# The order of the head in a fused state-space and SwiGLU kernel: when the first four row groups are normed, turned and sent through w1 and w3

## The chip, the cores and the metric

The kernel runs on one core of a Trainium2 chip. The metric is the device time of one execution in microseconds (us), as the median of three runs. A profile of one execution is read beside it.

The engines are named as in the profile: PE (TensorE, matmuls; PEld are its weight loads), DVE (VectorE), ACT (ScalarE), POOL (GpSimd), SP (SyncE, which here only issues DMAs). "L143" is line 143 of the kernel before.

## What is computed

```python
def _layernorm(x, axis=-1, eps=1e-5):
    m = jnp.mean(x, axis=axis, keepdims=True)
    v = jnp.var(x, axis=axis, keepdims=True)
    return (x - m) / jnp.sqrt(v + eps)

def reference(...):                      # x: 1 x 2048 x 512, bfloat16
    def _A_ref(x, ...):                  # diagonal complex state space, 512 states
        dt = jnp.exp(log_dt)
        Lam_bar = jnp.exp(dt * Lam)
        B_bar = ((Lam_bar - 1.0) / Lam)[:, None] * Bmat
        Bu = jnp.einsum("bld,pd->blp", x + 0j, B_bar)
        for t in range(L):
            h = Lam_bar[None, :] * h + Bu[:, t, :]
        ...
        return 2.0 * jnp.einsum("blp,dp->bld", hseq, Cmat).real + x * Dskip

    def _B_ref(x, w1, w3, w2):           # SwiGLU, 512 -> 1792 -> 512
        return (silu(x @ w1) * (x @ w3)) @ w2

    xn = _layernorm(x, axis=-1)
    return x + _A_ref(xn, ...) + _B_ref(xn, B_w1, B_w3, B_w2)
```

## The kernel before

The 2048 rows are cut into four blocks of 512 (`TBLK`), a block into four row groups of 128 (`CPB`; group c is "rows c" below). Every matmul needs the normed rows turned, with the 512 features on the partitions: `xnT` of a block is 128 x 4 x 512, where the 4 are the feature tiles (`NDT`).

The order of all engines' work is written out by hand (`manual_schedule`): each engine runs its instructions in the order of the text, and waits only for what they read or overwrite. From the second block on, VectorE's work stands in a queue of tasks with costs, and TensorE's loops call `drain(us)` to put as many of them between their own steps as fit. The norm of these blocks is such a task, and its turning is a transposing DMA.

Block 0 can't wait for that. Its head is the stretch that the change is about:

- SyncE's queue issues x of block 0 in three pieces (rows 0, rows 1, rows 2 and 3), then pieces of w1 and w3 (`load_w13`: f tiles 0 to 1, 2 to 3, 4 to 5, ...); the first w1 piece is on ScalarE's queue.
- `keep_warm` (L140) runs matmuls on a constant tile whose result nobody reads.
- For each row group: `stats` and `aggr` on VectorE (mean and variance), `rstd_act` on ScalarE (Ln, then Exp with -0.5: the reciprocal root), `normed` on VectorE (`xn`), `turn` on TensorE (four 128 x 128 transposes into PSUM), and `put`, which copies the turned rows out of PSUM into `xnT`, on ScalarE or VectorE.
- `ahead` (L491) runs the matmuls of the first three f tiles (`begun`: three gate and three up banks of PSUM) on those row groups that are there; a bank holds 512 rows of one f tile.
- `par_cols` (L256): TensorE turns the state-space parameters (`prm` into `pprm`), ScalarE copies them out and takes an Exp, GpSimd multiplies; then ScalarE takes `r_col` and loads the table that holds Silu (L527).

`glu_up(0)` (L361) then finishes the last 128 rows of the three begun f tiles, and goes on with f = 3 to 13 at the full width of 512 rows. For each f tile ScalarE takes Silu of the gate bank (`sl16`, L374) and copies the up bank (`up16`, L376), and VectorE multiplies them (L383). PSUM has eight banks, handed out in turn: the gate matmuls of f = 3 get the bank of the first begun tile and wait for its Silu. The first task that `glu_up(0)` drains is `par_turns` (L279), some 3 us of VectorE's work on the parameters.

The order of the head of before is L500 to L538, printed below.

Of the kernel before, what the change touches and what calls it, by code (L numbers as in the profile page):

```python
# [11 lines left out]
ALU = mybir.AluOpType  # L12
# [3 lines left out]
BF16 = DT.bfloat16  # L16
P = 128
# [3 lines left out]
def kernel(  # L21
# [24 lines left out]
    nc = tc.nc  # L46
    _, S, D = A_x.shape
# [5 lines left out]
    CPB = TBLK // P  # L53
    NSB = TBLK // SB
    NDT = D // P
    NPT = PS // P
# [7 lines left out]
    const = ctx.enter_context(tc.tile_pool(name="const", bufs=1))  # L64
    xpool = ctx.enter_context(tc.tile_pool(name="xpool", bufs=NBLK))
    work = ctx.enter_context(tc.tile_pool(name="work", bufs=2))
    psum = ctx.enter_context(tc.tile_pool(name="psum", bufs=8, space=bass.MemoryType.PSUM))
    ctx.enter_context(tc.manual_schedule())

    def ps_tile(name):  # L70
        return psum.tile([P, 512], FP32, name=name, tag="ps")


    x_blk = [xpool.tile([P, CPB, D], BF16, name="x_blk") for _ in range(NBLK)]
    for c0, c1 in ((0, 1), (1, 2), (2, CPB)):
        nc.sync.dma_start(out=x_blk[0][:, c0:c1, :], in_=xv[:, 0, c0:c1, :])
    w1_sb = const.tile([P, NDT, F], BF16, name="w1_sb")
    w3_sb = const.tile([P, NDT, F], BF16, name="w3_sb")
    w2_sb = const.tile([P, NFT, D], BF16, name="w2_sb")
    w1v = B_w1.rearrange("(t p) f -> p t f", p=P)  # L80
    w3v = B_w3.rearrange("(t p) f -> p t f", p=P)

    def load_w13(f0, f1, first=nc.sync):
        fs = slice(f0 * P, f1 * P)
        first.dma_start(out=w1_sb[:, :, fs], in_=w1v[:, :, fs])
        nc.sync.dma_start(out=w3_sb[:, :, fs], in_=w3v[:, :, fs])

    dskip_row = const.tile([P, D], BF16, name="dskip_row")
    bt = [const.tile([P, NDT, PS], BF16, name=f"bt{ri}") for ri in range(2)]
# [3 lines left out]
        for t in range(NDT):  # L93
            nc.sync.dma_start_transpose(out=dst[:, t, :], in_=src[:, t * P:(t + 1) * P])

    nc.scalar.preload_act_table_set("natural_log_exp_and_others")
    prm = const.tile([3 * NPT, P], BF16, name="prm")

    def load_prm(i, src, eng):
        eng.dma_start(out=prm[i * NPT:(i + 1) * NPT, :], in_=src.rearrange("(t p) -> t p", p=P))  # L100

    load_prm(0, A_Lambda_re, nc.scalar)
    load_prm(1, A_Lambda_im, nc.scalar)
    load_w13(0, 2, nc.scalar)
    load_prm(2, A_log_dt, nc.sync)
    load_w13(2, 4)
    load_w13(4, 6)
    nc.sync.dma_start(out=x_blk[1], in_=xv[:, 1, :, :])
    load_w13(6, 10)
# [10 lines left out]
        load_turned(ct[1], A_C_im)  # L120


    warm = const.tile([P, P], BF16, name="warm")
    nc.vector.memset(warm, 0.0)  # L124
    halfpi = const.tile([P, 1], FP32, name="halfpi")
    nc.vector.memset(halfpi, float(np.pi / 2))  # L126
    eps = const.tile([P, 1], FP32, name="eps")
# [1 line left out]
    ident = const.tile([P, P], BF16, name="ident")  # L129
# [5 lines left out]
    iota_f = const.tile([P, SB], FP32, name="iota_f")  # L135
    nc.gpsimd.tensor_copy(out=iota_f, in_=iota_i)

    wps = ps_tile("warm_ps")

    def keep_warm(n, width=512):  # L140
        rhs = warm.unsqueeze(1).to_broadcast([P, width // P, P])
        for _ in range(n):
            nc.tensor.matmul(out=wps[:, :width], lhsT=warm, rhs=rhs, start=True, stop=True)  # L143

    keep_warm(9)


    mv_all = const.tile([P, NBLK * CPB, 2], FP32, name="mv_all")
    rstd_all = const.tile([P, NBLK * CPB], FP32, name="rstd_all")
# [3 lines left out]
    def stats(c):  # L153
        sums[c] = work.tile([P, 6], FP32, name="stats", bufs=4)
        nc.vector.bn_stats(out=sums[c], in_=x_blk[c // CPB][:, c % CPB, :])  # L155

    def aggr(c):
        nc.vector.bn_aggr(out=mv_all[:, c, :], in_=sums.pop(c))

    def rstd_act(c0, c1):  # L160
        y = rstd_all[:, c0:c1]
        nc.scalar.activation(out=y, in_=mv_all[:, c0:c1, 1], func=ACT.Ln, bias=eps)
        nc.scalar.activation(out=y, in_=y, func=ACT.Exp, scale=-0.5)
# [12 lines left out]
            nc.vector.tensor_scalar(out=tmp, in0=tmp, scalar1=-0.5, scalar2=1.5, op0=ALU.mult, op1=ALU.add)  # L176
            nc.vector.tensor_tensor(out=y, in0=y, in1=tmp, op=ALU.mult)

    def normed(c):
        xn = work.tile([P, D], BF16, name="xn", bufs=8)  # L180
        nc.vector.tensor_scalar(out=xn, in0=x_blk[c // CPB][:, c % CPB, :], scalar1=mv_all[:, c, 0:1],
                                scalar2=rstd_all[:, c:c + 1], op0=ALU.subtract, op1=ALU.mult)
        return xn

    def residual(c, xn):
# [6 lines left out]
    def new_xnT(b):  # L192
        xnTs[b] = work.tile([P, NDT, TBLK], BF16, name="xnT", bufs=3)
# [8 lines left out]
    def ln_tasks(b):  # L202
        c0 = b * CPB
        xns = {}

        def first():
            new_xnT(b)
            stats(c0)

        def second(c):  # L210
            stats(c)
            aggr(c - 1)

        def scaled():
            aggr(c0 + CPB - 1)
            rstd(c0, c0 + CPB)

        def norm_one(c):
            xns[c] = normed(c)
            cl = c - c0  # L220
            nc.sync.dma_start_transpose(out=xnTs[b][:, :, cl * P:(cl + 1) * P], in_=xns[c])

        yield 0.7, first
        for c in range(c0 + 1, c0 + CPB):
            yield 0.8, lambda c=c: second(c)
        yield 2.5, scaled
        for c in range(c0, c0 + CPB):
            yield 0.42, lambda c=c: norm_one(c)
        xns_of[b] = xns


    new_xnT(0)
    pprm = psum.tile([P, 3 * NPT], BF16, name="prm_ps", tag="ps")
    xn0 = xns_of[0] = {}

    def turn(c, pxt, d0=0, d1=NDT):
        for dt in range(d0, d1):
            nc.tensor.transpose(out=pxt[:, dt - d0, :], in_=xn0[c][:, dt * P:(dt + 1) * P], identity=ident)  # L238

    def put(c, pxt, eng, d0=0, d1=NDT):  # L240
        dst = xnTs[0][:, d0:d1, c * P:(c + 1) * P]
        if eng is nc.scalar:
            nc.scalar.activation(out=dst, in_=pxt, func=ACT.Copy)
        else:
            nc.vector.tensor_copy(out=dst, in_=pxt)  # L245
# [6 lines left out]
    def c4(name):  # L252
        col[name] = const.tile([P, NPT], FP32, name=f"c_{name}")
        return col[name]

    def par_cols():  # L256
        prmc = const.tile([P, 3 * NPT], FP32, name="prmc")
        nc.scalar.activation(out=prmc, in_=pprm, func=ACT.Copy)
        col["lre"], col["lim"], col["ldt"] = (prmc[:, i * NPT:(i + 1) * NPT] for i in range(3))
        nc.scalar.activation(out=c4("dt"), in_=col["ldt"], func=ACT.Exp)  # L260
        nc.gpsimd.tensor_tensor(out=c4("kr"), in0=col["dt"], in1=col["lre"], op=ALU.mult)
        nc.gpsimd.tensor_tensor(out=c4("ki"), in0=col["dt"], in1=col["lim"], op=ALU.mult)
        nc.gpsimd.tensor_scalar(out=c4("turn"), in0=col["ki"], scalar1=float(1.0 / (2.0 * np.pi)), scalar2=None,
                                op0=ALU.mult)
        tt = nc.gpsimd.tensor_tensor
        tt(out=c4("den"), in0=col["lre"], in1=col["lre"], op=ALU.mult)
        tt(out=c4("d2"), in0=col["lim"], in1=col["lim"], op=ALU.mult)
        tt(out=col["den"], in0=col["den"], in1=col["d2"], op=ALU.add)
# [87 lines left out]
    def glu_mm(b, f, w_sb, ps, ts):  # L356
        for dt in range(NDT):
            nc.tensor.matmul(out=ps[:, ts], lhsT=w_sb[:, dt, f * P:(f + 1) * P], rhs=xnTs[b][:, dt, ts],  # L358
                             start=(dt == 0), stop=(dt == NDT - 1))
# [125 lines left out]
                nc.sync.dma_start(out=ov[:, c, ds], in_=o16[:, ds])  # L485


    def new_xt(n=NDT):
        return psum.tile([P, n, P], BF16, name="xt_ps", tag="ps")

    def ahead(fs, w_sbs, c0, c1):  # L491
        for f in fs:
            for w_sb in w_sbs:
                glu_mm(0, f, w_sb, begun[f][w_sb is w3_sb], slice(c0 * P, c1 * P))

    H = NDT // 2
    ta, tb, t1 = new_xt(H), new_xt(H), new_xt()
    begun = [(ps_tile("g_ps"), ps_tile("u_ps")) for f in range(3)]

    stats(0)  # L500
    aggr(0)
    rstd_act(0, 1)
    stats(1)
    xn0[0] = normed(0)
    aggr(1)
    rstd_act(1, 2)
    turn(0, ta, 0, H)
    turn(0, tb, H, NDT)
    keep_warm(4, P)
    put(0, ta, nc.scalar, 0, H)  # L510
    stats(2)
    put(0, tb, nc.vector, H, NDT)
    xn0[1] = normed(1)
    aggr(2)
    rstd_act(2, 3)
    stats(3)
    ahead((0, 1), (w1_sb,), 0, 1)
    turn(1, t1)
    put(1, t1, nc.vector)
    ahead((0, 1), (w3_sb,), 0, 1)  # L520
    nc.tensor.transpose(out=pprm, in_=prm, identity=ident[:3 * NPT, :3 * NPT])  # L521
    xn0[2] = normed(2)
    aggr(3)
    rstd_act(3, 4)
    par_cols()
    nc.scalar.activation(out=r_col, in_=col["kr"], func=ACT.Exp)
    nc.scalar.preload_act_table_set("silu_and_others")  # L527
    xn0[3] = normed(3)
    ahead((0, 1), (w1_sb, w3_sb), 1, 2)
    ahead((2,), (w1_sb,), 0, 2)  # L530
    t2, t3 = new_xt(), new_xt()
    turn(2, t2)
    put(2, t2, nc.vector)
    ahead((2,), (w3_sb,), 0, 2)
    ahead((0,), (w1_sb, w3_sb), 2, 3)
    turn(3, t3)
    put(3, t3, nc.scalar)
    ahead((1, 2), (w1_sb, w3_sb), 2, 3)  # L538

    push([(3.2, par_turns), (0.2, par_recip)])  # L540
    push([(0.0, lambda: for_act.extend(par_trig()))])
# [53 lines left out]
```

## Time and profile before

| what | value |
|---|---|
| median of three runs | 212.47 us (212.34 to 216.35) |
| the profiled execution | 212.5 us, of which 210.7 us are the span from first to last instruction |
| PE busy | 205.9 us, 98% of the span |
| DVE, ACT, POOL busy | 173.6 us (82%), 93.3 us (44%), 5.4 us (3%) |
| last matmul streamed | about 207.9 us after the span's start |

A row of the timeline reads: start, duration, engine, line, operation, output<-inputs, shapes, count, and in brackets how long the engine had been idle and what ended this. Neighbouring equal instructions are merged into one row, from the first one's start to the last one's end. Matmuls are pipelined: a row's duration holds the latency of its last one, so the pace is read from start to start. Times count from the span's start.

### The profile page before, as it was taken

The page shows a single profiled execution, that of the slowest core. Times are in us where ns is not written, and L with a number is a line of the kernel's source. Part 1 is how long each engine was busy: PE and PEld are TensorE (multiplying, and loading weights), DVE is VectorE, ACT ScalarE, POOL GpSimd, SP SyncE. Part 2 cuts the span into 40 slices and gives each one's busy share as a digit, 9 for nine tenths or more (in the row PEclk, how much of TensorE's full clock was granted, in tenths as well). Part 3 has the DMA queues.
Part 4 walks back from the last instruction along what each step waited for, and adds up shares of the span by engine and source line. Part 5 has one row for each costly group of instructions (what it writes and reads, how often), then busy time and mean ns, then how long its engine had stood idle before and what let it go on. Part 6 is the DMA issues. An engine that isn't in the chain of part 4 may idle for free.

```text
span 210.7 us, 2875 instructions
## 1 busy us (share of the span) xinstructions
PE 205.9 (98%) x1026; PEld 97.7 (46%) x1044; DVE 173.6 (82%) x345; ACT 93.3 (44%) x165; POOL 5.4 (3%) x27
## 2 busy tenths in 40 slices
PE   8999999999999999999999999999999999999994
PEld 3864444444444444444444444444444444444453
DVE  4889999988999999999999999999999999121111
ACT  4689866666666200066666600036666620000000
POOL 2200320000000000000000000000000000000000
PEclk9999999999999999999999999999999999999999
DMA  5999589964000000000002200100000000000110
GB/s 169 307 350 205 104 194 292 201 130 106 18 3 0 0 25 25 28 26 0 0 0 55 50 1 24 50 28 0 2 0 0 3 0 25 26 25 25 41 37 25
DMA packets 27094, 13.69 MB, mean 65 GB/s; under 512 B 15944, under 2 KB 27080, under 8 KB 27080
## 3 DMA queue, kind: packets, MB, share of 16 engines
q1 hardware_dynamic: 26536, 13.25, 26.7%
q10 hardware_dynamic: 544, 0.26, 0.5%
q8 instruction: 8, 0.13, 0.3%
q14 instruction: 6, 0.05, 0.1%
HBM read 7.74 MB, written 2.10 MB: 47 GB/s over the span
## 4 chain that ended last, share of the span: by engine, by line
PE 97%; ACT 1%; issue 1%; DVE 0%; ACTq 0%
PE u_ps L358 23%; PE y_ps L474 23%; PE g_ps L358 22%; PE y_ps L479 13%; PE bu_ps L397 13%; PE warm_ps L143 2%; ACT up L376 1%; PE xt_ps L238 1%; DVE xnT L245 0%; DVE o L484 0%; DVE warm L124 0%; PE prm_ps L521 0%; ACTq L376 0%; DVE eps L128 0%; DVE halfpi L126 0%
## 5 line engine op out<-in xcount | busy, mean ns | idle before, releaser
L358 PEld LDWEIGHTS <-w_sb 128*128 128x128 bf16 x512 | 46.7, 98 | 50.5 <-DMA w_sb<-in_B_w_dram 0.3
L358 PE MATMUL u_ps<-xnT,w_sb 128*128 128x512 bf16 (+2 forms) x255 | 58.7, 352 | 0.3
L358 PE MATMUL g_ps<-xnT,w_sb 128*128 128x512 bf16 (+2 forms) x249 | 57.8, 352 | 0.3
L474 PE MATMUL y_ps<-w_sb,hgT 128*128 128x512 bf16 (+2 forms) x233 | 50.7, 366 | 0.2
L376 ACT ACTIVATE up<-u_ps 128x512 bf16<-128x512 f32 x56 | 33.7, 602 | 15.8 <-PE u_ps L358 15.5
L399 ACT ACTIVATE u<-bu_ps 128x512 bf16<-128x512 f32 x32 | 19.1, 597 | 46.3 <-PE bu_ps L397 46.3
L374 ACT ACTIVATE sl<-g_ps 128x512 bf16<-128x512 f32 x56 | 33.7, 602 | 10.0 <-PE g_ps L358 8.9
L431 DVE TENSOR_TENSOR_SCAN ab<-r_col,h,ab 128x256 bf16<-128x256 f32 x56 | 37.6, 731 | 0.2
L474 PEld LDWEIGHTS <-hgT 128*128 128x128 bf16 x238 | 22.8, 98 | 25.9
L484 DVE TENSOR_TENSOR o<-y_ps,x_blk 128x512 bf16<-128x512 f32 (+2 forms) x17 | 11.1, 653 | 24.3 <-PE y_ps L479 24.3
L479 PE MATMUL y_ps<-ct,h 128*128 128x512 bf16 (+2 forms) x134 | 30.2, 366 | 0.1
L397 PE MATMUL bu_ps<-xnT,bt 128*128 128x512 bf16 x125 | 27.8, 379 | 0.2
L383 DVE TENSOR_TENSOR hgT<-sl,up 128x512 bf16<-128x512 bf16 x56 | 23.1, 414 | 3.3 <-ACT up L376 3.2
L479 PEld LDWEIGHTS <-h 128*128 128x128 bf16 x136 | 13.0, 98 | 14.7
L397 PEld LDWEIGHTS <-bt 128*128 128x128 bf16 x128 | 12.5, 97 | 15.2
L155 DVE BATCH_NORM_STATS2 stats<-x_blk 128x6 f32<-128x512 bf16 x16 | 10.6, 676 | 2.3 <-DMA x_blk<-in_A_x_dram 2.3
L440 DVE TENSOR_TENSOR ab<-ab,tab_s 128x2048 bf16<-128x2048 bf16 x8 | 9.8, 1222 | 0.2
L436 DVE TENSOR_TENSOR ab<-ab,tab_c 128x2048 bf16<-128x2048 bf16 x8 | 9.8, 1222 | 0.1
L416 DVE TENSOR_TENSOR ab<-u,tab_y 128x2048 bf16<-128x2048 bf16 x8 | 9.8, 1220 | 0.0
L413 DVE TENSOR_TENSOR ab<-u,tab_x 128x2048 bf16<-128x2048 bf16 x8 | 9.8, 1219 | 0.0
L190 DVE TENSOR_TENSOR x_blk<-xd,x_blk 128x512 bf16<-128x512 bf16 x16 | 6.8, 428 | 0.5
L189 DVE TENSOR_TENSOR xd<-xn,dskip_row 128x512 bf16<-128x512 bf16 x16 | 6.7, 418 | 0.0
(72 smaller groups left out, 79.5 us busy)
## 6 DMA issues: line engine op xcount, KB each, us to landing
w_sb<-in_B_w_dram SPq DMA_DIRECT2D x4, 512.0 KB, 7.2
out_dram<-o SPq DMA_DIRECT2D x15, 128.0 KB, 1.7
w_sb<-in_B_w_dram SPq DMA_DIRECT2D x1, 1792.0 KB
x_blk<-in_A_x_dram SPq DMA_DIRECT2D x3, 512.0 KB, 7.5
w_sb<-in_B_w_dram SPq DMA_DIRECT2D x5, 256.0 KB, 4.6
x_blk<-in_A_x_dram SPq DMA_DIRECT2D x2, 128.0 KB, 2.2
w_sb<-in_B_w_dram ACTq DMA_DIRECT2D x1, 256.0 KB, 4.2
x_blk<-in_A_x_dram SPq DMA_DIRECT2D x1, 256.0 KB, 3.5
```

Source lines behind the costliest of these rows:

```text
L155: nc.vector.bn_stats(out=sums[c], in_=x_blk[c // CPB][:, c % CPB, :])
L358: nc.tensor.matmul(out=ps[:, ts], lhsT=w_sb[:, dt, f * P:(f + 1) * P], rhs=xnTs[b][:, dt, ts], start=(dt == 0), stop=(dt == NDT - 1))
L374: nc.scalar.activation(out=sl16, in_=g_ps, func=ACT.Silu)
L376: nc.scalar.activation(out=up16, in_=u_ps, func=ACT.Copy)
L383: nc.vector.tensor_tensor(out=hg[b][:, f, :], in0=sl16, in1=up16, op=ALU.mult)
L397: nc.tensor.matmul(out=u_ps, lhsT=bt[ri][:, dt, pt * P:(pt + 1) * P], rhs=xnTs[b][:, dt, :], start=(dt == 0), stop=(dt == NDT - 1))
L399: nc.scalar.activation(out=u16[:, :, pt, ri, :], in_=u_ps.rearrange("p (s t) -> p s t", s=NSB), func=ACT.Copy)
L413: nc.vector.tensor_tensor(out=ab[0][:, :, 0:2, :], in0=u16, in1=tab_b("x"), op=ALU.mult)
L431: nc.vector.tensor_tensor_scan(out=a[:, pt, 2 * ri + 1, :], data0=r_b, data1=a[:, pt, 2 * ri, :], initial=init, op0=ALU.mult, op1=ALU.add)
L474: nc.tensor.matmul(out=y_ps[:, ds], lhsT=hg[b][:, f, cl * P:(cl + 1) * P], rhs=w2_sb[:, f, ds], start=(f == 0), stop=False)
L479: nc.tensor.matmul(out=y_ps[:, ds], lhsT=h_tiles[i][:, pt, ri, h_ts], rhs=ct[ri][:, pt, ds], start=False, stop=(pt == NPT - 1 and ri == 1))
L484: nc.vector.tensor_tensor(out=o16[:, ds], in0=y_ps[:, ds], in1=x_blk[b][:, cl, ds], op=ALU.add)
```

## The change

Order and places in the head, and little else:

- `keep_warm` multiplies a built-in constant, read with zero stride, in place of a zeroed tile, into a begun gate bank in place of a bank of its own; eight matmuls of 512 and two of 128 columns instead of nine of 512.
- `aggr(1)` and `rstd_act(1, 2)` come ahead of the norm of rows 0, which is done in two halves of 256 features.
- All of rows 0's turned features are copied by ScalarE; norm, turn and copy (ScalarE) of rows 1 come ahead of the statistics of rows 2 and ahead of every matmul with w1. The copy of rows 2 moves to ScalarE, that of rows 3 to VectorE.
- w1 of f tiles 0 and 1 is done for rows 0, then for rows 1; w3 of the same and all of f tile 2 for both (256 rows) at once. The parameters are turned after w1 of f tile 2.
- The PSUM tiles for turning: two banks (`xt_a`, `xt_b`), each holding two targets, instead of five tiles of their own (with the one for the parameters).
- In the text, the table preload of ScalarE moves up, and `load_w13` takes a pair of queues.

```diff
+    nc.scalar.preload_act_table_set("natural_log_exp_and_others")
...
-    def load_w13(f0, f1, first=nc.sync):
+    def load_w13(f0, f1, engs=(nc.sync, nc.sync)):
...
-    nc.scalar.preload_act_table_set("natural_log_exp_and_others")
...
-    load_w13(0, 2, nc.scalar)
+    load_w13(0, 2, (nc.scalar, nc.sync))
...
-    warm = const.tile([P, P], BF16, name="warm")
-    nc.vector.memset(warm, 0.0)
...
-    wps = ps_tile("warm_ps")
+    begun = [(ps_tile("g_ps"), ps_tile("u_ps")) for _ in range(3)]

     def keep_warm(n, width=512):
-        rhs = warm.unsqueeze(1).to_broadcast([P, width // P, P])
+        one = nc.const_aps.tensor_like(1.0, like=ident[:, 0:1])
         for _ in range(n):
-            nc.tensor.matmul(out=wps[:, :width], lhsT=warm, rhs=rhs, start=True, stop=True)
-
-    keep_warm(9)
+            nc.tensor.matmul(out=begun[0][0][:, :width], lhsT=one.to_broadcast([P, P]), rhs=one.to_broadcast([P, width]),
+                             start=True, stop=True)
+
+    keep_warm(8)
+    keep_warm(2, P)
...
-    def normed(c):
+    def normed(c, parts=1):
         xn = work.tile([P, D], BF16, name="xn", bufs=8)
-        nc.vector.tensor_scalar(out=xn, in0=x_blk[c // CPB][:, c % CPB, :], scalar1=mv_all[:, c, 0:1],
-                                scalar2=rstd_all[:, c:c + 1], op0=ALU.subtract, op1=ALU.mult)
+        for i in range(parts):
+            ds = slice(i * D // parts, (i + 1) * D // parts)
+            nc.vector.tensor_scalar(out=xn[:, ds], in0=x_blk[c // CPB][:, c % CPB, ds], scalar1=mv_all[:, c, 0:1],
+                                    scalar2=rstd_all[:, c:c + 1], op0=ALU.subtract, op1=ALU.mult)
         return xn
...
-    pprm = psum.tile([P, 3 * NPT], BF16, name="prm_ps", tag="ps")
+    xt_a = psum.tile([P, 2 * NDT, P], BF16, name="xt_ps", tag="ps")
+    xt_b = psum.tile([P, 2 * NDT, P], BF16, name="xt_ps", tag="ps")
+    pprm = xt_a[:, NDT, :3 * NPT]
...
-    def ahead(fs, w_sbs, c0, c1):
+    def ahead(w_sbs, fs, c, n=1):
         for f in fs:
             for w_sb in w_sbs:
-                glu_mm(0, f, w_sb, begun[f][w_sb is w3_sb], slice(c0 * P, c1 * P))
+                glu_mm(0, f, w_sb, begun[f][w_sb is w3_sb], slice(c * P, (c + n) * P))

     H = NDT // 2
-    ta, tb, t1 = new_xt(H), new_xt(H), new_xt()
-    begun = [(ps_tile("g_ps"), ps_tile("u_ps")) for f in range(3)]
+    ta, tb, t1, t2, t3 = xt_a[:, :H], xt_b[:, :H], xt_a[:, NDT:], xt_b[:, NDT:], xt_a[:, :NDT]
```

The order of the head after the change, from `stats(0)` to the start of the queue:

```python
    stats(0)
    aggr(0)
    rstd_act(0, 1)
    stats(1)
    aggr(1)
    rstd_act(1, 2)
    xn0[0] = normed(0, 2)
    turn(0, ta, 0, H)
    put(0, ta, nc.scalar, 0, H)
    xn0[1] = normed(1)
    turn(0, tb, H, NDT)
    put(0, tb, nc.scalar, H, NDT)
    keep_warm(2, P)
    turn(1, t1)
    put(1, t1, nc.scalar)
    keep_warm(4, P)
    stats(2)
    aggr(2)
    rstd_act(2, 3)
    stats(3)
    ahead((w1_sb,), (0, 1), 0)
    ahead((w1_sb,), (0, 1), 1)
    xn0[2] = normed(2)
    aggr(3)
    rstd_act(3, 4)
    ahead((w3_sb,), (0, 1), 0, 2)
    turn(2, t2)
    put(2, t2, nc.scalar)
    xn0[3] = normed(3)
    ahead((w1_sb,), (2,), 0, 2)
    nc.tensor.transpose(out=pprm, in_=prm, identity=ident[:3 * NPT, :3 * NPT])
    par_cols()
    ahead((w3_sb,), (2,), 0, 2)
    ahead((w1_sb, w3_sb), (0,), 2)
    turn(3, t3)
    put(3, t3, nc.vector)
    nc.scalar.activation(out=r_col, in_=col["kr"], func=ACT.Exp)
    nc.scalar.preload_act_table_set("silu_and_others")
    ahead((w1_sb, w3_sb), (1, 2), 2)
```

More of the change, by code (lines that the diff above doesn't have):

```diff
@@ L81 @@
     w3v = B_w3.rearrange("(t p) f -> p t f", p=P)
-    def load_w13(f0, f1, first=nc.sync):
+    def load_w13(f0, f1, engs=(nc.sync, nc.sync)):
         fs = slice(f0 * P, f1 * P)
-        first.dma_start(out=w1_sb[:, :, fs], in_=w1v[:, :, fs])
-        nc.sync.dma_start(out=w3_sb[:, :, fs], in_=w3v[:, :, fs])
+        engs[0].dma_start(out=w1_sb[:, :, fs], in_=w1v[:, :, fs])
+        engs[1].dma_start(out=w3_sb[:, :, fs], in_=w3v[:, :, fs])
     dskip_row = const.tile([P, D], BF16, name="dskip_row")
@@ L485, in y_out @@
                 nc.sync.dma_start(out=ov[:, c, ds], in_=o16[:, ds])
-    def new_xt(n=NDT):
-        return psum.tile([P, n, P], BF16, name="xt_ps", tag="ps")
-    def ahead(fs, w_sbs, c0, c1):
+    def ahead(w_sbs, fs, c, n=1):
         for f in fs:
             for w_sb in w_sbs:
-                glu_mm(0, f, w_sb, begun[f][w_sb is w3_sb], slice(c0 * P, c1 * P))
+                glu_mm(0, f, w_sb, begun[f][w_sb is w3_sb], slice(c * P, (c + n) * P))
     H = NDT // 2
-    ta, tb, t1 = new_xt(H), new_xt(H), new_xt()
-    begun = [(ps_tile("g_ps"), ps_tile("u_ps")) for f in range(3)]
+    ta, tb, t1, t2, t3 = xt_a[:, :H], xt_b[:, :H], xt_a[:, NDT:], xt_b[:, NDT:], xt_a[:, :NDT]
     stats(0)
@@ L503 @@
     stats(1)
-    xn0[0] = normed(0)
     aggr(1)
     rstd_act(1, 2)
+    xn0[0] = normed(0, 2)
     turn(0, ta, 0, H)
+    put(0, ta, nc.scalar, 0, H)
+    xn0[1] = normed(1)
     turn(0, tb, H, NDT)
+    put(0, tb, nc.scalar, H, NDT)
+    keep_warm(2, P)
+    turn(1, t1)
+    put(1, t1, nc.scalar)
     keep_warm(4, P)
-    put(0, ta, nc.scalar, 0, H)
     stats(2)
-    put(0, tb, nc.vector, H, NDT)
-    xn0[1] = normed(1)
     aggr(2)
@@ L516 @@
     stats(3)
[L517 to L521, printed above, removed]
+    ahead((w1_sb,), (0, 1), 0)
+    ahead((w1_sb,), (0, 1), 1)
     xn0[2] = normed(2)
@@ L524 @@
     rstd_act(3, 4)
+    ahead((w3_sb,), (0, 1), 0, 2)
+    turn(2, t2)
+    put(2, t2, nc.scalar)
+    xn0[3] = normed(3)
+    ahead((w1_sb,), (2,), 0, 2)
+    nc.tensor.transpose(out=pprm, in_=prm, identity=ident[:3 * NPT, :3 * NPT])
     par_cols()
+    ahead((w3_sb,), (2,), 0, 2)
+    ahead((w1_sb, w3_sb), (0,), 2)
+    turn(3, t3)
+    put(3, t3, nc.vector)
     nc.scalar.activation(out=r_col, in_=col["kr"], func=ACT.Exp)
     nc.scalar.preload_act_table_set("silu_and_others")
[L528 to L538, printed above, removed]
+    ahead((w1_sb, w3_sb), (1, 2), 2)
     push([(3.2, par_turns), (0.2, par_recip)])
```

## The prediction

> **What bounds the kernel now.** I read the page first, then the timeline of the first 17 us, then that stretch one matmul at a time (narrow windows of the timeline), then the DMA view issue by issue.
>
> ```profile
> PE 205.9 (98%) x1026; PEld 97.7 (46%) x1044; DVE 173.6 (82%) x345; ACT 93.3 (44%) x165; POOL 5.4 (3%) x27
> ...
> PE 97%; ACT 1%; issue 1%; DVE 0%; ACTq 0%
> ```
>
> TensorE is 98% busy and 97% of the chain that ended last. So the end moves by what TensorE loses or saves in the head, unless a later wait takes it back. Matmul by matmul I find no start later than its predecessor's stream by over 12 ns between 9.70 us and the last matmul at 207.9. All idle time that can be saved lies in front of that:
>
> ```profile
> 0.97 4.02 PE L143 MATMUL warm_ps<-warm 128*128 128x512 bf16 x9 [0.97 <-DVE eps L128]
> ...
> 4.37 0.41 DVE L181 TENSOR_SCALAR xn<-x_blk,mv_all,rstd_all 128x512 bf16<-128x512 bf16 x1
> 4.70 0.17 DVE L158 BATCH_NORM_AGGREGATE mv_all<-stats 128x2 f32<-128x6 f32 x1
> 4.84 0.61 PE L238 MATMUL xt_ps<-ident,xn 128*128 128x128 bf16 x4
> 5.21 0.69 DVE L155 BATCH_NORM_STATS2 stats<-x_blk 128x6 f32<-128x512 bf16 x1 [0.34 <-DMA x_blk<-in_A_x_dram]
> 5.23 0.20 ACT L163 ACTIVATE rstd_all<-rstd_all 128x1 f32<-128x1 f32 x1
> 5.24 0.63 PE L143 MATMUL warm_ps<-warm 128*128 128x128 bf16 x4
> 5.34 0.36 ACT L243 ACTIVATE xnT<-xt_ps 128x256 bf16<-128x256 bf16 x1
> 5.82 0.27 DVE L245 COPY xnT<-xt_ps 128x256 bf16<-128x256 bf16 x1
> 5.88 0.76 PE L358 MATMUL g_ps<-xnT,w_sb 128*128 128x128 bf16 x8
> 6.01 0.41 DVE L181 TENSOR_SCALAR xn<-x_blk,mv_all,rstd_all 128x512 bf16<-128x512 bf16 x1
> 7.00 0.41 DVE L245 COPY xnT<-xt_ps 128x512 bf16<-128x512 bf16 x1
> 9.22 0.43 DVE L245 COPY xnT<-xt_ps 128x512 bf16<-128x512 bf16 x1 [0.39 <-PE xt_ps L238]
> 9.23 1.28 ACT L527 ACT_TABLE_LOAD   x1
> 9.70 0.38 PE L358 MATMUL g_ps<-xnT,w_sb 128*128 128x128 bf16 x4
> 10.57 0.60 ACT L243 ACTIVATE xnT<-xt_ps 128x512 bf16<-128x512 bf16 x1
> 11.68 0.60 ACT L374 ACTIVATE sl<-g_ps 128x512 bf16<-128x512 f32 x1 [0.52 <-PE g_ps L358]
> 12.60 1.03 PE L358 MATMUL g_ps<-xnT,w_sb 128*128 128x512 bf16 x3
> 13.46 1.03 PE L358 MATMUL u_ps<-xnT,w_sb 128*128 128x512 bf16 x4
> ```
>
> The ruler is 12.60, where f = 3, the first full-width group, begins. From there groups of four follow each other evenly (13.46, 14.33, ...: 0.864 us, 216 ns a matmul). In front of it TensorE's array stands still five times: 5.67 to 5.88 (the first w1 piece, issued 1.63, landed 4.2 later), 6.00 to 6.15 (second half of xnT for rows 0, copied by VectorE at 5.82 because stats(2) stood ahead of it), 6.71 to 6.79 (w3 piece, 2.12 + 4.6), 7.25 to 7.46 apart from some 0.05 of the parameter transpose (xnT of rows 1, copied 7.00 to 7.41), 9.46 to 9.70 (xnT of rows 2). That is 0.21 + 0.15 + 0.08 + 0.16 + 0.24 = 0.84.
>
> The rows also show a slow array at first: nine 512-wide warm-up matmuls start 427 ns apart, and four 128-wide ones at 5.24 start 107 ns apart; from 5.95 on the spacings are 56 ns (128 wide), 109 (256), 216 (512). The page's granted clock reads full throughout, so the turn is seen in the spacing alone, between 5.67 and 5.95.
>
> **The change, part by part.**
>
> *Warm-up.* Nine matmuls of 427 ns become 8 x 427 + 2 x 107 = 3.63 us. They no longer wait for VectorE's memsets (released 0.95); the other engines begin at 0.71 to 0.80, so I put the start at 0.75 and the end at 4.4. The turn waits for rows 0 anyway: worth nothing, hidden by the x load and the statistics (first xn at 4.78). What before does not show is the constant read with zero stride: between the 427 ns spacing and 634 ns, the whole duration of one such matmul by itself (by the 128-wide row, 314), which gives 0.75 + 8 x 0.634 + 2 x 0.314 = 6.45 and costs 1.6. I take 427: same width, same engine.
>
> *Preload and loads.* The table load moves up in the text, but ScalarE's stream has it first either way, and every DMA keeps its queue and place: nothing. Landings stay: w1 f0-1 5.84, w3 f0-1 6.75, w1 f2-3 7.64, w3 f2-3 8.55.
>
> *Aggregate 1 ahead of norm 0.* stats(1) ends 4.35, aggr(1) starts 4.38, norm(0) follows 0.10 later (aggr(0) to stats(1): 3.59 to 3.69) at 4.48 where it was 4.37. It is now two halves. A 256-wide copy takes 0.27 against 0.41, so a half norm is 0.41 - 0.13 = 0.28 and follows in 0.33 - 0.13 = 0.20: halves end 4.76 and 4.96. The first transposes start about 4.82, the last two 5.04 and 5.14: as before within 0.03. In exchange ScalarE's Ln for rows 1 starts 4.59 instead of 4.91, so rstd(1) is there at 5.13, not 5.44.
>
> *Copies of rows 0, both on ScalarE.* First half 5.28 to 5.64; the second follows 0.26 later, 5.54 to 5.90. VectorE ended it at 6.09.
>
> *Norm 1 and turn 1 first.* VectorE has no copy and no stats(2) in the way: norm(1) runs 5.15 to 5.55 (was 6.01). turn(1) could start 5.61. Its target now shares the bank xt_a with the half that ScalarE reads until 5.64; before, each had its own, so no row shows such a wait: bounds 5.61 and 5.69, and I take 5.69. The array turning fast on the way, the transposes stream until 5.91 and end 6.13. put(1) takes 0.60 on ScalarE (the row at 10.57; VectorE's 0.41 is given up): 6.15 to 6.75, matmuls on rows 1 from 6.80 (was 7.46). Behind put(1) on ScalarE stand Ln and Exp of rows 2 (6.64 to 7.17), then norm(2) 7.19 to 7.59: still ahead of turn(2).
>
> [...]
>
> *TensorE from there.* keep_warm(4) (0.22) and w1 of rows 0 (8 x 56 = 0.45) fill 5.91 to 6.58; 0.22 idle. Then, counted from 6.80: w1 rows 1 0.45; w3 f0-1 at 256 rows 8 x 109 = 0.87; turn(2) 0.22; w1 f2 0.44; parameters 0.11; w3 f2 0.44; f0 rows 2 0.45; turn(3) 0.22; f1-2 rows 2 0.90; the last 128 rows of f0-2, 24 x 56 = 1.34. Sum 5.44: f = 3 at 12.24. (256 at once hardly saves streaming: 109 against 2 x 56, 12 pairs, 0.04.)
>
> *Waits on the way.* w3 f2 begins 8.89, landed 8.55. Rows 2: turn(2) 8.12, put(2) 8.55 to 9.15, needed 9.33: slack 0.14. Rows 3: turn(3) 9.78, put(3) on VectorE 10.19 to 10.62, needed 10.90: 0.25. ScalarE then has the parameters (9.04), dt (9.23), r_col behind GpSimd's product (9.76) and the 1.28 table load until 11.27; sl(0) 11.31 to 11.91, and f = 3 reuses its bank at 12.24: slack 0.29. Behind put(3) VectorE begins the turns at 10.5 (was 9.56), so the products start about 13.75 (was 12.80); sl16 has four buffers, and sl(4) is not due until about 15.6.
>
> **Sum**: 12.60 - 12.24 = 0.36 saved. The profiled execution took 212.5 (span 210.7 and 1.8 around it), beside a median of 212.47. Forecast **212.1**. Its own range is 211.8 to 212.4: a slack that fails costs up to 0.3, a wait that I doubled gives 0.1 to 0.3 back.
>
> **The rivals.**
>
> *The array turns fast later (slower than before).* TensorE now stands still from 4.4 to 4.82 and from 5.46 to 5.69, just before the turn; before, it stood still 0.06 us up to 5.67. For: 427 to 216 ns came only after 4.7 to 5.0 us of nearly unbroken matmuls. Against: 3.6 us of them stay, and the start is earlier. If the count began anew at 4.82 and took 4.7 again, full speed comes at 9.5. At double spacing turn(1) to rows 0 last until 7.40, rows 1 until 8.25, w3 f0-1 until about 9.73 instead of 8.12. That is 1.6 late: f = 3 at 13.85, total 213.7. It decides from a turn at about 6.8 on; earlier than that the change still gains.
>
> [...]
>
> *The gain turns into a wait for ScalarE.* It gets two copies of VectorE's (0.36 and 0.60) and loses one, and everything behind the table load is in order. For: slacks of 0.14 and 0.29 only. Against: it stands idle 0.3 to 0.8 us four times in the old head. With the load 0.6 later sl(0) ends 12.5 and f = 3 starts where it did: 212.5.
>
> *The halves bring nothing.* If the transposes wait for the whole xn (4.96), everything up to put(1) comes about 0.15 later: f = 3 at 12.39, 212.3.
>
> **How the numbers follow.** Forecast 0.62, ScalarE's wait 0.12, halves 0.10 (both inside or just beside the forecast's range), late turn 0.14, the slow constant 0.02. The range 211.7 to 213.0 leaves out the two last and little more. Within 2% (4.2 us, about what a measurement of this kernel tells from no change, its runs spanning 212.34 to 216.35) are all of these cases; beyond it only unknown ones: faster 0.01, same 0.96, slower 0.03.
>
> **What would show it.** Right: second put of rows 0 on ScalarE ending near 5.9, norm(1) at 5.15, rows 1 streamed from 6.8, no array gap over 0.1 after that, f = 3 at 12.2, the same 216 ns cadence to the end. Wrong: 107 ns spacing of 128-wide matmuls after 6 us; a gap in front of f = 3 that ends with ScalarE; a gap after 13 us that before did not have.

## The result, and the profile after

| | median | runs | middle half of the runs |
|---|---|---|---|
| before | 212.91 us | 22 | 212.45 to 213.47 |
| after | 212.26 us | 22 | 212.20 to 212.34 |

The ratio of after to before is 0.9966, 95% interval 0.995 to 0.9982: 0.4 to 1.1 us faster, so within 2%. (The ratio leaves disturbed runs out.) What stands out is the width: the middle half of before spreads over a whole microsecond, that of after over 0.14. The fastest runs are nearly alike: 212.16 before, 212.09 after.

The profiled execution of after took 212.21 us, its span is 210.4. The first view is its page, shares of the span and of the chain that ended last; the second its timeline, with the columns as before. (L143 is again the warm-up, L244 the turn, L249 and L251 the copies by ScalarE and VectorE, L364 the w1 and w3 matmuls, L380 Silu.)

```profile
PE 206.4 (98%) x1039; PEld 97.6 (46%) x1039; DVE 172.9 (82%) x343; ACT 94.4 (45%) x167; POOL 5.8 (3%) x27
...
PE 96%; DVE 1%; DMA 1%; ACT 0%; issue 0%
```

```profile
0.76 3.79 PE L143 MATMUL g_ps<-const-bfloat16-1.0 128*128 128x512 bf16 x10 [0.76 <-PEq L581]
...
4.84 0.56 PE L244 MATMUL xt_ps<-ident,xn 128*128 128x128 bf16 x4 [0.30 <-DVE xn L185]
...
5.27 0.66 ACT L249 ACTIVATE xnT<-xt_ps 128x256 bf16<-128x256 bf16 x2 [0.16 <-PE xt_ps L244]
...
5.47 0.69 DVE L157 BATCH_NORM_STATS2 stats<-x_blk 128x6 f32<-128x512 bf16 x1
...
5.71 0.38 PE L244 MATMUL xt_ps<-ident,xn 128*128 128x128 bf16 x4 [0.19 <-ACT xnT L249]
...
6.12 0.60 ACT L249 ACTIVATE xnT<-xt_ps 128x512 bf16<-128x512 bf16 x1 [0.20 <-PE xt_ps L244]
...
6.16 1.22 PE L364 MATMUL g_ps<-xnT,w_sb 128*128 128x128 bf16 x16
...
7.22 1.04 PE L364 MATMUL u_ps<-xnT,w_sb 128*128 128x256 bf16 x8
...
8.85 0.18 PE L532 MATMUL xt_ps<-ident,prm 12*128 12x12 bf16 x1
...
10.34 0.42 DVE L251 COPY xnT<-xt_ps 128x512 bf16<-128x512 bf16 x1 [1.65 <-PE xt_ps L244]
...
11.39 0.60 ACT L380 ACTIVATE sl<-g_ps 128x512 bf16<-128x512 f32 x1
...
12.30 1.03 PE L364 MATMUL g_ps<-xnT,w_sb 128*128 128x512 bf16 x4
...
13.17 1.03 PE L364 MATMUL u_ps<-xnT,w_sb 128*128 128x512 bf16 x4
```

f = 3 begins at 12.30 instead of 12.60, and the groups follow each other 0.86 apart as before. What to see: stats(2) at 5.47 no longer waits for a DMA, as its x piece landed at 4.88; before it had waited in front of TensorE's work. Behind 6.16 the array stands still twice, 0.17 at 6.60 (in the merged row, waiting for rows 1) and 0.10 in front of the parameter transpose at 8.85.

The two profiled executions differ by 0.30 at f = 3 and by 0.3 in the span (210.7 and 210.4), the medians by 0.65. The profile that the prediction was made from took 212.5, less than 15 of the 22 runs of before, so the question is what else the change takes away, in the other executions.

### The profile page after: what moved, and what is told of

The parts are those of the page before. It is cut to its first block, busy times and chain, and to the rows that moved or that the text cites. A ratio compares the mean times of both kernels' runs of the same rounds, so it can differ in the third digit from the quotient of the medians.

```text
span 210.4 us, 2883 instructions
## 1 busy us (share of the span) xinstructions
PE 206.4 (98%) x1039; PEld 97.6 (46%) x1039; DVE 172.9 (82%) x343; ACT 94.4 (45%) x167; POOL 5.8 (3%) x27
## 4 chain that ended last, share of the span: by engine, by line
PE 96%; DVE 1%; DMA 1%; ACT 0%; issue 0%
PE g_ps L364 23%; PE u_ps L364 23%; PE y_ps L480 23%; PE y_ps L485 13%; PE bu_ps L403 13%; DMA x_blk<-in_A_x_dram 1%; DVE stats L157 1%; PE xt_ps L244 1%; ACT xnT L249 0%; DVE mv_all L160 0%; DVE o L490 0%; DVE xn L185 0%; PE g_ps L143 0%; PE xt_ps L532 0%
## 5 line engine op out<-in xcount | busy, mean ns | idle before, releaser
L364 PEld LDWEIGHTS <-w_sb 128*128 128x128 bf16 x504 | 46.5, 98 | 50.1
L364 PE MATMUL g_ps<-xnT,w_sb 128*128 128x512 bf16 (+1 forms) x256 | 58.5, 352 | 0.0
L364 PE MATMUL u_ps<-xnT,w_sb 128*128 128x512 bf16 (+2 forms) x248 | 58.4, 358 | 0.0
L380 ACT ACTIVATE sl<-g_ps 128x512 bf16<-128x512 f32 x56 | 33.7, 602 | 9.9 <-PE g_ps L364 9.1
L185 DVE TENSOR_SCALAR xn<-x_blk,mv_all,rstd_all 128x512 bf16<-128x512 bf16 (+1 forms) x17 | 6.1, 401 | 1.0 <-ACT rstd_all L165 0.8
```

What stands on the lines that cost most here:

```text
L380: nc.scalar.activation(out=sl16, in_=g_ps, func=ACT.Silu)
```

## The experiments

In all kernels of the experiments plain DMAs of the same bytes stand in for the transposing ones, from about 11.9 us on, behind the head (so the state-space matrices and the later blocks' rows are not turned). "Plain before" and "plain change" are the yardsticks. Each set of four ran on one chip beside the kernel before, a chip of its own for each set; most kernels have twelve runs, a_nowarm six, a_split1 nine, b_noall eleven. "Landed" is a DMA's issue plus its time to landing, "array turned" is when 107 ns spacing of 128-wide matmuls became 56 ns, or 427 ns of 512-wide ones 216.

| run | median | middle half | ratio to before (95%) | f = 3 in its profile |
|---|---|---|---|---|
| b_plain | 212.45 | 212.36 to 212.75 | 0.9983 (0.9961 to 1.0004) | 13.43 |
| a_plain | 212.16 | 212.15 to 212.32 | 0.9971 (0.9959 to 0.9983) | 12.22 |
| b_newwarm | 212.62 | 212.48 to 212.89 | 0.9998 (0.9979 to 1.0017) | 12.75 |
| a_oldwarmup | 212.24 | 212.20 to 212.41 | 0.9978 (0.9965 to 0.999) | 12.51 |
| b_nowait | 212.55 | 212.36 to 212.71 | 0.9987 (0.9965 to 1.0009) | 12.32 |
| a_stats2first | 212.77 | 212.59 to 214.05 | 1.0025 (1.0003 to 1.0048) | 14.23 |
| a_ownbank | 212.19 | 212.14 to 212.38 | 0.9985 (0.9972 to 0.9997) | 12.30 |
| a_nowarm | 213.98 | 213.59 to 214.16 | 1.006 (1.0039 to 1.0081) | 14.47 |
| b_noland | 212.55 | 212.19 to 212.72 | 0.9993 (0.998 to 1.0005) | 12.20 |
| b_noall | 212.40 | 212.19 to 212.52 | 0.9987 (0.9976 to 0.9998) | 12.49 |
| a_noall | 212.32 | 212.29 to 212.35 | 0.9986 (0.9976 to 0.9997) | 12.28 |
| a_split1 | 211.91 | 211.83 to 212.13 | 0.9968 (0.9955 to 0.998) | 12.22 |

Before had 212.66, 212.51 and 212.58 beside the three sets.

In all fourteen profiled executions, before and after included, the time is that of f = 3 plus 199.9 us (199.89 to 199.93). From f = 3 on they all take equally long, so a run's time also tells, as an estimate, when its f = 3 began.

**First set: the yardsticks, and is it the warm-up?** Two theories for the width of before: the moment when the array turns fast ("clock"), or the moments when x, w1 and w3 land ("landing").

b_plain:

> The kernel before with its 28 transposing DMAs replaced by plain DMAs of the same bytes: B, C and the later blocks' rows are not turned (this part of the computation is left out, here and in every kernel below). The first of these DMAs is issued at 11.9 us, behind the head, so it is the yardstick of before: ratio to before 1.00 within 0.005, f = 3 near 12.6. Both theories want its spread. 22 runs of before went from 212.2 to 213.7 (two above that), those of the change only from 212.1 to 212.6. [...] Theory 'landing' (the spread is when the w1 and w3 pieces land, for which this order waits): the same spread, but f = 3 follows the landings of w1 f0-1 (5.84 in the first profile) and w3 f0-1 (6.75).

a_plain:

> The change with the same plain DMAs: the yardstick of after. Against the plain kernel before 0.3 to 0.7 us less, spread within 0.5 us, f = 3 at 12.3. If the difference to before vanished, the gain would have to do with the transposing DMAs behind the head, which neither theory says.

b_newwarm:

```diff
-    warm = const.tile([P, P], BF16, name="warm")
-    nc.vector.memset(warm, 0.0)
...
+        one = nc.const_aps.tensor_like(1.0, like=ident[:, 0:1])
...
-    keep_warm(9)
+    keep_warm(8)
+    keep_warm(2, P)
```

> The plain kernel before with the new warm-up alone (constant operand, no wait for VectorE, 8 of 512 and 2 of 128 columns; into its own bank). Theory 'clock': the start 0.2 us earlier narrows the spread to about 0.5 us and the median falls by 0.2 to 0.4, f = 3 stays near 12.6. Theory 'landing': nothing changes, median and spread as the plain kernel before in the same rounds (within 0.2).

a_oldwarmup:

```diff
+    warm = const.tile([P, P], BF16, name="warm")
+    nc.vector.memset(warm, 0.0)
...
-    keep_warm(8)
-    keep_warm(2, P)
+    keep_warm(9)
```

> The plain change with the old warm-up (zeroed tile, nine of 512 columns, start behind VectorE's memsets at 0.97). Theory 'clock': the spread of the kernel before returns, median 0.2 to 0.5 above the plain change; f = 3 at 12.3 in executions in which the array is fast by 5.7. Theory 'landing': median and spread as the plain change (within 0.1), since w1 is first read at 6.16 and w3 at 7.22, both well behind their landings.

The new warm-up in before made no difference clear of the spread (212.62 beside 212.45 for plain before and 212.66 for before), the old one in the change little (212.24 beside 212.16), as "landing" said. So the kind of warm-up and its start 0.2 us earlier are not the cause. They don't fix when the array turns fast, though (the last matmul at full slow spacing started anywhere from 2.84 to 6.30, more on this below), so what speaks against "clock" are the next two profiles: in both the array was fast before w1 was there, and f = 3 came late all the same. The profile of plain before caught the longest of its twelve executions (213.35 us). Its timeline:

```profile
5.26 0.39 PE L143 MATMUL warm_ps<-warm 128*128 128x128 bf16 x4
...
6.00 0.29 PE L358 MATMUL g_ps<-xnT,w_sb 128*128 128x128 bf16 x2 [0.35 <-DMA w_sb<-in_B_w_dram]
...
6.05 0.69 DVE L155 BATCH_NORM_STATS2 stats<-x_blk 128x6 f32<-128x512 bf16 x1 [1.05 <-DMA x_blk<-in_A_x_dram]
...
6.66 0.27 DVE L245 COPY xnT<-xt_ps 128x256 bf16<-128x256 bf16 x1
6.85 0.40 DVE L181 TENSOR_SCALAR xn<-x_blk,mv_all,rstd_all 128x512 bf16<-128x512 bf16 x1
6.99 0.49 PE L358 MATMUL g_ps<-xnT,w_sb 128*128 128x128 bf16 x6 [0.71 <-DVE xnT L245]
...
7.55 0.61 PE L358 MATMUL u_ps<-xnT,w_sb 128*128 128x128 bf16 x8
```

Read it from the end: TensorE stands still for VectorE's copy (it did two matmuls and had no second half of xnT). The copy was ready to go at 5.5, but VectorE takes its work in order, and stats(2) in front of it waited for the third x piece until 6.03. The array was already fast here (four warm-ups in 0.39 at 5.26).

The timeline of b_newwarm shows the other landings. TensorE starts 0.2 earlier and the array is fast by 5.07 (0.39 for four). Then TensorE stands still until w1 has landed (6.00), and again, after the transposes of rows 1, until w3 has (6.90):

```profile
0.76 3.65 PE L141 MATMUL warm_ps<-const-bfloat16-1.0 128*128 128x512 bf16 x10 [0.76 <-PEq L579]
...
5.07 0.39 PE L141 MATMUL warm_ps<-const-bfloat16-1.0 128*128 128x128 bf16 x4
6.05 0.70 PE L358 MATMUL g_ps<-xnT,w_sb 128*128 128x128 bf16 x8 [0.58 <-DMA w_sb<-in_B_w_dram]
6.59 0.39 PE L238 MATMUL xt_ps<-ident,xn 128*128 128x128 bf16 x4
6.95 0.23 PE L358 MATMUL u_ps<-xnT,w_sb 128*128 128x128 bf16 x1
```

(The last row is the first of eight; the view ends there.) The row of the kernel before is the same wait, for a w3 piece that landed at 6.75:

```profile
6.79 0.62 PE L358 MATMUL u_ps<-xnT,w_sb 128*128 128x128 bf16 x8
```

The third x piece landed at 5.19 in the first profile, at 5.30 in b_newwarm's and at 6.03 in plain before's; f = 3 began at 12.60, 12.75 and 13.43. That looks like one for one, and the next set was built on it. But only in the third profile was it the x piece that decided. In the other two it was w3: f = 3 follows the first w3 matmul by 5.81 (12.60 - 6.79) and 5.80 (12.75 - 6.95).

**Second set: the wait of stats(2), the bank, the clock's price.**

b_nowait:

```diff
-        nc.vector.bn_stats(out=sums[c], in_=x_blk[c // CPB][:, c % CPB, :])
+        src = 1 if c == 2 else c
+        nc.vector.bn_stats(out=sums[c], in_=x_blk[src // CPB][:, src % CPB, :])
```

> The plain kernel before, with one read changed: stats(2) takes x of rows 1 instead of rows 2 (so the statistics of rows 2 are left out). Every instruction and its order stay; only its wait for the third x piece goes. Three profiles of before have that piece landing at 5.19, 5.30 and 6.03 and f = 3 beginning at 12.60, 12.75 and 13.43: one for one. Theory 'stats(2) in front' (VectorE stands in front of the copy and norm that TensorE needs until that piece lands, and the change puts them ahead of it): stats(2) starts 4.8, f = 3 at 12.2 to 12.5 whatever the landing, median 212.1 to 212.4, spread under 0.6. Rival 'TensorE's order' (the gain comes from 256 rows at once and from rows 1 being ready before w1 is started): median stays 212.4 to 212.7 and the spread over 1 us.

A miss: the median stayed (212.55 beside 212.51). None of its twelve runs is above 213.1, where 5 of the 31 of before beside it are; that fits a wait which makes the longest times and not the usual ones, but twelve runs don't prove it. What the expectation had wrong shows in the kernel's own profile: with the wait for x gone, w3 decides. It landed early (6.46), the first w3 matmul started at 6.51, and f = 3 came 5.81 later, at 12.32.

a_stats2first:

```diff
+    stats(2)
     xn0[1] = normed(1)
...
-    stats(2)
     aggr(2)
```

> The plain change with stats(2) moved in front of the norm of rows 1 on VectorE, nothing else. Theory 'stats(2) in front': the norm of rows 1 follows the landing of the third x piece by 0.6; with landings of 4.7 to 6.0 rows 1 are streamed from 6.9 to 8.2 instead of 6.8, f = 3 at 12.4 to 13.7, median about 212.8, spread over 1 us. Rival 'TensorE's order': at most 0.2 above the plain change (212.16), spread within 0.5.

The median was as expected, 0.6 above the plain change (and above a_ownbank, on the same chip) for one instruction moved, but the profiled execution (214.15 us) shows a second reason that neither theory named. x had landed at 4.74, and norm(1) began only 0.3 later than in the change. TensorE's timeline:

```profile
5.92 0.61 PE L244 MATMUL xt_ps<-ident,xn 128*128 128x128 bf16 x4 [0.31 <-DVE xn L185]
6.32 0.63 PE L143 MATMUL g_ps<-const-bfloat16-1.0 128*128 128x128 bf16 x4
6.75 1.91 PE L364 MATMUL g_ps<-xnT,w_sb 128*128 128x128 bf16 x16
8.45 1.73 PE L364 MATMUL u_ps<-xnT,w_sb 128*128 128x256 bf16 x8
10.02 0.39 PE L244 MATMUL xt_ps<-ident,xn 128*128 128x128 bf16 x4
```

Sixteen matmuls took 1.91 where they take 1.22 in the change with a wait of 0.17 inside: the last matmul at full slow spacing started at 9.52. So the prediction's rival, the array turning fast late, is real. Three of the twelve runs lie at 214.05 and above, about 1.6 us over the other nine (mean 214.27 against 212.71); that the two that were not profiled are the same case is likely, not shown. It struck where TensorE stood still longer before turn(1): from 5.40 to 5.92, where the change has 5.35 to 5.71. Whether that is why isn't shown by a test of its own.

a_ownbank:

```diff
-    ta, tb, t1, t2, t3 = xt_a[:, :H], xt_b[:, :H], xt_a[:, NDT:], xt_b[:, NDT:], xt_a[:, :NDT]
+    ta, tb, t2, t3 = xt_a[:, :H], xt_b[:, :H], xt_b[:, NDT:], xt_a[:, :NDT]
+    t1 = begun[2][1].bitcast(BF16)[:, :NDT * P].rearrange("p (t q) -> p t q", t=NDT)
```

> The plain change with the turned rows 1 in a bank of their own (the up bank of f tile 2, unused until 8.9) instead of in xt_a, which ScalarE still reads. If the transposes of rows 1 waited for the bank: they start 5.61 instead of 5.7, f = 3 up to 0.1 earlier, time 0.05 to 0.1 lower. If they waited for something else: no difference.

In the profile of the change turn(1) was released by ScalarE's copy out of the same bank (row 5.71). With a bank of its own it started 0.06 after the end of norm(1) (5.63 to 5.69). But so it did in the plain change's profile (5.55 to 5.61), where the array was fast early (by 4.1) and the copy had ended at 5.53. In these profiles the wait is there only when the array turns fast later, at about 5.2 in the change, and the time didn't move (212.19 beside 212.16). Its price can be read all the same: counted from the landing of the first x piece (2.79 to 2.89), f = 3 comes 9.41 later in a_plain and a_ownbank, and 9.49 later in the change and in a_noall below, where turn(1) starts just behind the copy.

a_nowarm:

```diff
-    keep_warm(8)
-    keep_warm(2, P)
```

> The plain change without the ten warm-up matmuls in front (the six narrow ones further on stay): what the late turn of the array costs, the prediction's rival. TensorE then begins at 4.84, and if the array needs some 3.5 to 5 us of work from there, it is fast at 8.4 to 9.8; work from 5.7 on runs at half pace until then, 1.2 to 2.0 us lost: f = 3 at 13.5 to 14.3, time 213.4 to 214.2. If the pace in the head were not decided by the warm-up: 212.2.

Within what was expected in time (213.98). f = 3 came at 14.47, a little later than expected, since the array turned only about 10.5, some 5.6 us behind its first matmul at 4.94.

**Third set: the landings of w1 and w3 as well, and a quicker version.**

b_noland:

```diff
+    def head_mm(f, w_sb, ps, ts):
+        if f == 2:
+            return glu_mm(0, f, w_sb, ps, ts)
+        for dt in range(NDT):
+            nc.tensor.matmul(out=ps[:, ts], lhsT=x_blk[0][:, 0, dt * P:(dt + 1) * P], rhs=xnTs[0][:, dt, ts],
+                             start=(dt == 0), stop=(dt == NDT - 1))
...
-                glu_mm(0, f, w_sb, begun[f][w_sb is w3_sb], slice(c0 * P, c1 * P))
+                head_mm(f, w_sb, begun[f][w_sb is w3_sb], slice(c0 * P, c1 * P))
```

> The plain kernel before, in which the head's matmuls for f tiles 0 and 1 read x of rows 0 as their stationary operand in place of w1 and w3 (so these products are left out; shapes, count and order stay). TensorE no longer waits for the first w1 and w3 pieces, whose landings went from 5.45 to 6.00 and from 6.33 to 6.90 in the profiles; stats(2) still waits for the third x piece. Theory 'weights land late': median falls from 212.5 to about 212.3, spread still with a tail above 212.9 (the x piece). Theory 'x alone': no change, which the run without the wait for x (212.55, tail gone but median where it was) already speaks against.

b_noall is b_noland with b_nowait's edit:

> Both at once in the plain kernel before: no wait for x rows 2 in stats(2), none for w1 and w3 of f tiles 0 and 1. Theory 'landings' (x, w1 and w3 together make the difference between the two orders): 212.0 to 212.2 and within 0.4, as fast as the change, f = 3 at 12.1 to 12.3. Rival 'clock' (what is left is when the array turns fast): stays at 212.4 or above with a spread of 0.6 or more.

a_noall is the plain change with both edits:

> The same two substitutions in the plain change. Theory 'landings': nothing to remove, since w1 is first read at 6.16, w3 at 7.22 and stats(2) stands behind norm(1): median within 0.06 of the plain change (212.16), f = 3 at 12.2 to 12.3. If it fell by 0.1 or more, the change too is bound by a landing.

Taking the weights alone away left the median (212.55 beside 212.58), though the lower quarter came down to 212.19. Both together brought 212.40, with no run above 212.65, where 7 of the 33 of before beside it are above 212.9. The change with the same edits has 212.32 on the same chip. So the two orders are 0.08 apart, and their middle halves overlap; the plain kernels stood 0.29 apart, with middle halves that don't. Two expectations missed here. The gain of b_noall is smaller than the 212.0 to 212.2 expected. And a_noall, expected within 0.06 of the plain change, lies 0.16 above it, measured on another chip; part of the 0.29 closed from that side, and why isn't shown.

The profiled execution of b_noall took 212.40, its median. In it a wait has moved up that nobody had counted:

```profile
6.47 0.61 PE L496 MATMUL u_ps<-xnT,x_blk 128*128 128x128 bf16 x8
7.25 0.16 PE L529 MATMUL prm_ps<-ident,prm 12*128 12x12 bf16 x1 [0.17 <-DMA prm<-in_A_log_dt_dram]
7.34 0.40 PE L496 MATMUL g_ps<-xnT,x_blk 128*128 128x128 bf16 x4
```

Eight matmuls from 6.47 stream until 6.92, and the parameter transpose stands in TensorE's order until the log_dt piece is there: the array stands still for 0.33 in front of 7.25, where the other profiles of before's order have 0.10. Without these 0.24 f = 3 would have come at about 12.25, which by the sum above is 212.15, about the plain change's median. In the old order that transpose comes at 7.3, in the new one at 8.85. Behind it, the wait of 0.24 for xnT of rows 2 is in every profile of before's order.

a_split1, a version meant to be faster:

```diff
+    ta, tb, t2, t3 = xt_a[:, :H], xt_b[:, :H], xt_b[:, NDT:], xt_a[:, :NDT]
+    t1a, t1b = (begun[2][i].bitcast(BF16)[:, :H * P].rearrange("p (t q) -> p t q", t=H) for i in range(2))
...
-    keep_warm(2, P)
+    keep_warm(4, P)
...
-    keep_warm(2, P)
-    turn(1, t1)
-    put(1, t1, nc.scalar)
-    keep_warm(4, P)
+    keep_warm(3, P)
+    turn(1, t1a, 0, H)
+    turn(1, t1b, H, NDT)
+    put(1, t1a, nc.scalar, 0, H)
     stats(2)
+    put(1, t1b, nc.vector, H, NDT)
     aggr(2)
```

> A version meant to be faster: the plain change with the turned rows 1 in two unused begun banks, copied out half by ScalarE and half by VectorE (behind stats(2)) instead of whole by ScalarE (0.60); the four narrow warm-ups behind turn(1) go, and three more are put into gaps before it. Rows 1 can be streamed from 6.5 instead of 6.77, f = 3 at 12.0 to 12.05, time 211.9 to 212.0. It will be less if w1's landing (up to 6.0) or w3 f2-3's (up to 8.7, needed at about 8.7) becomes the wait, or if the array turns late for want of warm-up work.

The time came as expected: 211.91, 0.25 below the plain change and 0.4 below a_noall on its own chip; by the sum above, f = 3 at 12.01. The profiled execution lies above the median (212.13, f = 3 at 12.22): the array turned at 6.4, behind the first w1 matmul (6.10), and w1 itself had landed only at 6.05. The two halves do leave PSUM side by side:

```profile
6.12 0.38 ACT L249 ACTIVATE xnT<-g_ps 128x256 bf16<-128x256 bf16 x1
...
6.33 0.29 DVE L251 COPY xnT<-u_ps 128x256 bf16<-128x256 bf16 x1
...
7.13 1.04 PE L364 MATMUL u_ps<-xnT,w_sb 128*128 128x256 bf16 x8
```

Even so the w3 matmuls start at 7.13, as in the plain change's profile, where the array was fast by 4.1, and before the 7.22 of the change.

## Why the prediction was right, and what it missed

The forecast of 212.1, no change beyond 2%, held: 212.26 measured, inside the range and inside the likeliest case's own. The time came out because the sum was made of the new head's own rows, and these were read rightly; the saving did not come out, as shown further on. Step by step:

- *Warm-up*: started 0.76 (said 0.75), same 427 ns with the constant. No gain seen in before (b_newwarm).
- *Halves*: 0.31 and 0.34 rather than 0.28; first transposes 4.84 and 5.09 (said 4.82, 5.04), and they did start on the first half.
- *Copies and turn(1)*: second copy ended 5.93 (5.90), norm(1) ran 5.15 to 5.56 (5.15 to 5.55), turn(1) 5.71 with ScalarE's copy out of the same bank as its releaser (5.69), rows 1 streamed from 6.77 (6.80). No row of before shows the 0.08 for the shared bank that is in the 5.69; it was the author's choice of the later bound. In its place the change showed 0.09: norm(1) ended 5.56, and turn(1) came 0.15 behind it, where a_ownbank and the plain change have 0.06.
- *TensorE from there*: 12.30 - 6.77 = 5.53, said 5.44. The term that was mis-sized is the parameter transpose: 0.20 between its neighbours (8.75 to 8.95), of which 0.10 stood still in front of it (as in before, 7.25 to 7.34), where the sum had 0.11.
- *Waits on the way*: none, as said. Copy of rows 2 at 8.51 (8.55), of rows 3 at 10.34 (10.19), Silu at 11.39 (11.31), products at 13.72 (13.75).
- *Rivals*: ScalarE never became the wait, the halves worked. The late turn didn't strike the change with its full price in its 22 runs, of which none is above 212.57; a_stats2first shows that it can strike, and a_nowarm what it costs without a warm-up (1.8 over the plain change).

What failed is the baseline, "Landings stay", and with it the saving of 0.36. 12.60 was taken as the f = 3 of before, but it is that of one execution. The third x piece landed between 4.66 and 6.03 in the profiles, w1 between 5.44 and 6.05, w3 between 6.33 and 6.95, in kernels that issue them in the same order and within 0.1 us of the same times. The old order uses w1, w3 and the parameters as they land, and VectorE's copy and norm stand behind the statistics of the x piece. So its f = 3 lay at 12.60, 12.75 and 13.43 in the three profiles with these waits in place, and at 12.20 in b_noland's, where weights were not waited for and x landed at 4.71. The new order needs stats(2) late, w1 at 6.16, w3 at 7.22, the parameters at 8.85: f = 3 stayed between 12.22 and 12.30 in all four profiles of its order with the warm-up of the change in place, x from 4.66 to 5.23. (With the old warm-up 12.51, as the array turned at about 6.2.) It has little room at w1 alone, which landed at 6.05 at the latest, and follows the first x piece, whose landing varied least (2.73 to 2.96). The forecast saved 0.36, the two profiled executions show 0.30, the medians 0.65. With nothing late the two orders are about equally fast (b_noland 12.20, a_plain 12.22, and the fastest runs): what the change takes away is the price of late pieces.

That a landing decides is shown by the profiles: in each of the three, TensorE's last stop ahead of the w3 matmuls ends with one, w3 itself or, through VectorE, the third x piece. The experiments agree: with the wait for x gone w3 decided (b_nowait's profile), with both gone the log_dt piece (b_noall's), and there the gap to the change was 0.08 instead of 0.29. How much each landing makes of the 0.65 is not shown. The 0.65 is itself no fixed size, as before was at 212.51 to 212.66 beside the three sets and at 212.91 here; that median means f = 3 at about 13.0, and no such execution was profiled. Six of its 22 runs are above 213.4, later than any profile of its order; a still later piece or a late turn may have made them. Why the pieces land at such different times wasn't tried.

The moment at which the array turns fast spreads widely: with a warm-up from 0.76 or 0.97 on, the last matmul at full slow spacing started anywhere from 2.84 (a_ownbank) to 6.30 (a_split1), a spread of 3.5, and in the profile of a_stats2first at 9.52, 3.2 behind the latest of these. No run shows what sets it.

## What to carry to other kernels

Read a wait for a DMA as a range, not as a duration: one profile shows one landing (the third x piece here landed from 4.66 to 6.03), and an order that uses each piece as it lands pays for every late one (f = 3 from 12.60 to 13.43), while an order that puts work on data already there in front of it doesn't (12.22 to 12.30 with the warm-up of the change). On an engine that works in order, look at what stands behind an instruction that waits for a transfer (in plain before VectorE's copy, ready to go at 5.5, ran at 6.66 behind stats(2)), and move what the bottleneck needs ahead of it. The spread of the runs says as much of such a change as the median, and when one wait is removed and the median stays, look for the next.

## What the hardware showed that was not expected

- The same 256 KB x transfer, issued at the same 1.63 us (1.62 to 1.64), landed from 4.66 to 6.03.
- The granted clock reads full (1.00 from 5.2 to 5.7 us in before) where matmuls of 128 columns start 107 ns apart; the pace was to be read from the starts.
- With nearly the same dense warm-up from 0.76 on, the last matmul at full slow spacing started 2.1 us after the first (2.84, a_ownbank) or 5.5 us after it (6.30, a_split1).
